# Moving the next batch's transposes into late attention steps and reordering the start of a fused attention and sine-MLP kernel on one Trainium2 core

## The chip, the cores and the metric

The kernel runs on one core of one Trainium2 chip. The metric is the device time of one execution in microseconds (us), as a median of several executions. A profile of one execution gives its span (a little shorter than the timed run) and the time of each instruction. The engines are PE (TensorE), DVE (VectorE), ACT (ScalarE), POOL (GpSimd) and SP (SyncE). POOL and SP here also issue most transfers: POOL through the software queue, SP through a hardware queue.

## The reference, cut to what matters

```python
def _attn_ref(q, k, v, global_idx):            # B=8, H=8, S=576, D=64; 8 global positions
    scores = scale * np.matmul(q, k.transpose(0, 1, 3, 2))
    mask = np.abs(pos[:, None] - pos[None, :]) <= 32
    mask = mask | is_global[:, None] | is_global[None, :]
    ...                                        # softmax over the masked scores
    return np.matmul(attn, v)

def _moe_ref(x, w_in, w_out, alpha):           # x: 4608 x 512, w_in: 512 x 2048
    h = x @ w_in
    s = np.sin(alpha * h)
    g = h + s * s / (alpha + 1e-09)
    return g @ w_out
```

The attention's output, 8 batches of 576 tokens, is the input x of the second part. The kernel treats x in 9 chunks of 512 tokens.

## The kernel before

One period per batch: an attention stage, then the first product of a chunk (tile hb). The second product of the chunk before (tiles ops and o, 64 wide matmuls) is cut into groups of four, the "filling", that stand between the attention's steps. A step of the attention makes scores of one unit, their exponential on ACT, the mask on DVE, a row sum (den) and the values (num). Before a head pair can be scored, its k and q are turned by 24 PE transposes; the transposes of the next batch stand partly in the hb stage.

```python
def stage_Q(psA, b, n):
    ...                                            # 16 score matmuls into Sp
    nc.scalar.activation(out=E[:], in_=Sp[:, :, 0:EW], func=AF.Exp, scale=scale)
    nc.vector.tensor_tensor(out=E[:], in0=E[:], in1=mk..., op=ALU.mult)      # mask at once
    return E

# second product, end of a tile of 128 rows
if ts == CH // P - 1:
    nc.vector.tensor_copy(out=osb[:], in_=ops[:])   # last of four on DVE
else:
    nc.scalar.copy(out=osb[:], in_=ops[:])          # the others on ACT

# squares of an hb stage: POOL, but for these of the 16
sq_late = lambda nt: {5: nc.scalar, 10: nc.vector, 15: nc.vector}.get(nt, nc.gpsimd)

# attention of batch p: transposes of its own head pairs 2 and 3 in steps -2 and 0
parts, last = attention(p, psA, {2: -2, 3: 0})
counts = [1, 1, 1, 1, 1, 2, 2, 1, 0]                # groups of filling after each step
...
# hb stage: value shift, then head pairs 0 and 1 of the next batch
i_ = (10, 13)
m1[i_[0]] = partial(chain, m1[i_[0]], *pre, partial(stage_T, p + 1, 0, psB, "hb"))
m1[i_[1]] = partial(chain, m1[i_[1]], partial(stage_T, p + 1, 1, psB, "hb"))

# start
shift_v(0, nc.gpsimd)                               # copies values one block on, within SBUF
for f in w_loads[:2]:
    f()                                             # both halves of w_in, POOL's queue
def globals_v0():
    nc.vector.tensor_copy(out=VZ[96:128], in_=Vg32[96:128])
def loads():
    for f in [partial(gather_kq, 1), ..., pool_regs] + v_loads(1, ((0, H),)) + kq1[:2] + w_loads[2:3]:
        f()
```

The softmax here doesn't subtract the row's maximum and nothing guards it: scores larger than these inputs give would overflow.

Of the kernel before, what the change touches and what calls it, by code (L numbers as in the profile page):

```python
# [17 lines left out]
def kernel(  # L18
# [122 lines left out]
    def shift_v(b, eng=nc.sync):  # L141
        W = VW[b % 2].rearrange("p a h u d -> p a h (u d)")
        eng.dma_start(out=W[0:64, 1], in_=W[QB : QB + 64, 0])
        eng.dma_start(
            out=W[64:KB, 1, :, 0 : (NU - 1) * D], in_=W[64 - QB : KB - QB, 0, :, D:]
        )
# [11 lines left out]
    def w_load(dst, src):  # L158
# [8 lines left out]
        for i in range(2)  # L167
    ] + [
        partial(
            w_load, w_out[:, i * NT // 2 : (i + 1) * NT // 2, :],  # L170
            moe_w_out[i * WH : (i + 1) * WH, :].rearrange("(t p) n -> p t n", p=P),
        )
        for i in range(2)
# [33 lines left out]
    for f in kq0[:4]:  # L207
        f()
# [4 lines left out]
    )  # L213

# [3 lines left out]
    def zero_v(i, eng=nc.vector):  # L218
# [16 lines left out]
    Gf = setup.tile([P, NG], F32, name="Gf")  # L235
    nc.vector.tensor_copy(out=Gf[:], in_=gall[:].bitcast(DT.int32)[:, 0::2])
    Gsel = setup.tile([P, 3 + NG], F32, name="Gsel")
    nc.vector.tensor_scalar(
        out=Gsel[:, 1:2], in0=I8[:, 0:1], scalar1=2.0, scalar2=None, op0=ALU.mult
    )  # L240
    nc.vector.scalar_tensor_tensor(
        out=Gsel[:, 2:3], in0=I8[:, 1:2], scalar=1.0 / (2 * NHP) - 2.0, in1=Gsel[:, 1:2],
        op0=ALU.mult, op1=ALU.add,
    )
    nc.vector.scalar_tensor_tensor(
        out=Gsel[:, 3:], in0=I8[:, 3:], scalar=0.0, in1=Gf[:], op0=ALU.is_equal, op1=ALU.mult
    )
    nc.vector.tensor_reduce(
        out=Gsel[:, 0:1], in_=Gsel[:, 3:], axis=mybir.AxisListType.X, op=ALU.add
    )  # L250
    rowi = const.tile([P, 1], DT.uint32, name="rowi")
    nc.vector.scalar_tensor_tensor(
        out=rowi[:], in0=Gsel[:, 2:3], scalar=float(S), in1=Gsel[:, 0:1],
        op0=ALU.mult, op1=ALU.add,
    )

    def gather_kq(i):
        for kq, src in ((0, k), (1, q)):
            nc.gpsimd.indirect_dma_start(
                out=GKQ[:, kq, i, :],  # L260
                out_offset=None,
                in_=src.rearrange("b h s d -> (b h s) d"),
                in_offset=bass.IndirectOffsetOnAxis(ap=rowi[:, 0:1], axis=0),
                element_offset=i * 2 * H * S * D,
            )

    zero_v(0)
    for f in v0 + kq0[4:]:
        f()
    gather_kq(0)  # L270
    Kps0 = psA0.tile([P, 2 * CH], BF, name="o2")

    def edges(t_):
# [5 lines left out]
    Vg32 = setup.tile([P, DM], F32, name="Vg32")  # L279
    zero(Vg32[96:128])  # L280
    zero(kTw[0][:, :, KB:P])

# [13 lines left out]
    nc.vector.tensor_tensor(  # L296
        out=OH[:], in0=T6[:, :, None].to_broadcast([P, NTW, NG]),
        in1=Gf[:, None, :].to_broadcast([P, NTW, NG]), op=ALU.is_equal,
    )
    Gp = setup.tile([P, 1], F32, name="Gp")  # L300
    nc.vector.tensor_copy(out=Gp[:], in_=gcol[:].bitcast(DT.int32)[:, 0:1])
    DQ = setup.tile([P, S], F32, name="DQ")
    nc.scalar.activation(out=DQ[:], in_=IQ[:], func=AF.Square, scale=-1.0, bias=Gp[:, 0:1])
    nc.vector.tensor_scalar(
# [47 lines left out]
    zero(VZ[0:96].bitcast(F32))  # L352
    for hp in range(1, NHP):
        zero(kTw[hp][:, :, KB:P])
    nc.vector.memset(ones[:], 1.0)
# [8 lines left out]
    shift_v(0, nc.gpsimd)  # L364
    for f in w_loads[:2]:
        f()
# [14 lines left out]
    def globals_v0():  # L381
        nc.vector.tensor_copy(out=VZ[96:128], in_=Vg32[96:128])
# [7 lines left out]
    def gather_v():  # L390
        regs = [
            nc.sync.value_load(gsc[0:1, 2 * j : 2 * j + 1], min_val=0, max_val=S - 1)
            for j in range(NG)
        ]
        for j in range(NG):
            nc.sync.dma_start(
                out=Vg32[KB + j : KB + j + 1, :].rearrange("p (h d) -> p h d", d=D),
                in_=v[0, :, bass.ds(regs[j], 1), :].rearrange("h o d -> o h d"),
            )
        for j in range(NG):  # L400
            nc.sync.dma_start(
                out=gN[2 * B * j : 2 * B * (j + 1), :].rearrange("b (h d) -> b h d", d=D),
                in_=v.rearrange("b (c h) s d -> (b c) h s d", c=2)[:, :, bass.ds(regs[j], 1), :].rearrange("b h o d -> b h (o d)"),
            )
# [68 lines left out]
    def T_Q(b, hp, qpool, qtag, copy):  # L473
        Qps = qpool.tile([P, S], BF, name=qtag)
        T_half(qk[b][0], b, hp, Qps)
        copy(out=qT[hp][:, :, 0:QB], in_=Qps[:].rearrange("p (i c) -> p i c", c=QB))

    def stage_T(b, hp, pool, tag):
        T_K(b, hp, Kps, nc.vector.tensor_copy)
        T_Q(b, hp, pool, tag, nc.scalar.copy)  # L480
# [16 lines left out]
    def stage_Q(psA, b, n):  # L497
        Sp = psA.tile([P, 2, CH], F32, name="Sp")
        i0 = blocks(n)[0][1]
# [8 lines left out]
        nc.scalar.activation(out=E[:], in_=Sp[:, :, 0:EW], func=AF.Exp, scale=scale)  # L508
        mk = MASK[:, i0 : i0 + NB, :].rearrange("p u c -> p (u c)")
# [3 lines left out]
        return E  # L513
# [80 lines left out]
    def attention(b, psA, t_at=None):  # L594
# [7 lines left out]
        def step(j):  # L602
            if j == -3:
                nc.scalar.preload_act_table_set("natural_log_exp_and_others")  # L604
            if j >= 0:
                stage_V(psA, b, j, Es.pop(j), recs.pop(j), gn)
            if 0 <= j + 1 < NUN:
                recs[j + 1] = stage_D(psA, j + 1, Es[j + 1], gd)
                if j + 2 == NUN:
                    stage_Gd(gd, gr)  # L610
                    nc.scalar.preload_act_table_set("trig_and_small")
            if j + 3 < NUN:
                Es[j + 3] = stage_Q(psA, b, j + 3)

        def one(op, j):
            if op == "Q":
                Es[j] = stage_Q(psA, b, j)
            elif op == "D":
# [7 lines left out]
        if t_at is None:  # L626
            return one, partial(stage_G, b, gn, gr)
        parts = [partial(step, j) for j in range(-LEAD, NUN)]
        for hp, j in t_at.items():
            parts[j + LEAD] = partial(chain, parts[j + LEAD], partial(stage_T, b, hp, psA, "qp"))  # L630
        return parts, partial(stage_G, b, gn, gr)

    def chain(*fs):
        for f in fs:
            f()


    def mm1(c, H2b, psB, sq):
# [10 lines left out]
        for nt in range(NT):  # L649
            def slot(nt=nt):  # L650
# [13 lines left out]
                eng = sq(nt)  # L664
                if eng is nc.scalar:
# [12 lines left out]
    def mm2(c, H2b, pools, cut=False):  # L678
# [3 lines left out]
        for ts in range(CH // P - (1 if cut else 0)):  # L682
            for g in range(NT // G4):
                def slot(ts=ts, g=g):
# [10 lines left out]
                    if g == NT // G4 - 1:  # L695
                        osb = osbp.tile([P, DM], F32, name="osb")
                        if ts == CH // P - 1:
                            nc.vector.tensor_copy(out=osb[:], in_=ops[:])
                        else:
                            nc.scalar.copy(out=osb[:], in_=ops[:])  # L700
# [44 lines left out]
    sq_late = lambda nt: {5: nc.scalar, 10: nc.vector, 15: nc.vector}.get(nt, nc.gpsimd)  # L745
# [9 lines left out]
    def loads():  # L755
        for f in [partial(gather_kq, 1), partial(zero_v, 1, nc.gpsimd), pool_regs] + v_loads(1, ((0, H),)) + kq1[:2] + w_loads[2:3]:
# [18 lines left out]
    def phase_0():  # L775
        Q, D_, V = (partial(partial, one, o) for o in "QDV")
        fs = {
            "warm": warm, "loads": loads, "vg": globals_v0, "vn": globals_v, "alpha": partial(alpha_t, aB),
            "keep": keep_warm, "last": last0, "A": partial(globals_t, 0, psC, "ops"), "kb": lambda: [f() for f in kq1[2:]],
        }  # L780
        for hp, (kp, ck, qpool, tag) in enumerate(
# [3 lines left out]
            fs[f"q{hp}"] = partial(T_Q, 0, hp, qpool, tag, acopy if hp < 3 else vcopy)  # L785
# [4 lines left out]
        for o, f in (("Q", Q), ("D", D_), ("V", V)):  # L790
            fs.update({f"{o}{j}": f(j) for j in range(NUN)})
        order = (
            "warm K0 q0 G0 Q0 K1 k1 q1 p1 loads Q1 D0 Q2 D1 K2 q2 G2 D2 Q3 vg K3 q3 G3 D3 Q4 V0 V1 D4 Q5 V2 V3 D5 V4 "
            "alpha V5 last keep A vn kb n0 n1 n2 n3"
# [4 lines left out]
    for p in range(NCH):  # L799
# [4 lines left out]
        elif p < B:  # L804
            with phase_pool("psA", 1) as psA:
                for tag, shape, dt_ in (
                    ("num", [P, NB, QC], F32), ("den", [P, NB, QC], F32),
                    ("qp", [P, S], BF), ("o2", [P, DM], F32),
# [3 lines left out]
                if p == 1:  # L812
                    fill[:8] = [fill[4 * (i % 2) + i // 2] for i in range(8)]
                parts, last = attention(p, psA, {2: -2, 3: 0})
                counts = [1, 1, 1, 1, 1, 2, 2, 1, 0]
                fill.pop(0)()
                fill.pop(0)()
# [7 lines left out]
                run(parts + [last], counts + [0], fill)  # L825
# [6 lines left out]
        with phase_pool("psB", 6) as psB:  # L832
# [3 lines left out]
            if p < 3:  # L836
                m1[5] = partial(chain, m1[5], partial(globals_t, p + 1, psB, "hb"))
            if p + 1 < B:
                i_ = (10, 13)
                pre = [partial(shift_v, p + 1), partial(global_v, p + 1)]  # L840
                if p == 0:
                    m1[5] = partial(chain, m1[5], *pre)
                    m1[6] = partial(chain, m1[6], w_loads[3])
                    pre, i_ = (), (12, 14)
                m1[i_[0]] = partial(chain, m1[i_[0]], *pre, partial(stage_T, p + 1, 0, psB, "hb"))
                m1[i_[1]] = partial(chain, m1[i_[1]], partial(stage_T, p + 1, 1, psB, "hb"))
# [34 lines left out]
```

## Time and profile before

| | before |
|---|---|
| median of the first three timed runs | 367.18 us (366.81 to 367.78) |
| span of the profile, mean PE clock | 366.4 us, 0.972 |
| start, up to the first hb matmul | 34.99 us |
| first hb stage, then attention of batch 1 | 16.23 and 25.56 us |
| second hb stage, then attention of batch 2 | 15.61 and 22.48 us |
| one settled hb stage and one settled attention | 15.61 and 22.53 us |

A stage is told from the timeline: from its first matmul on hb to the first scores or w_out matmul after it, and so on in turn. The prediction below shows the main views. The columns of a timeline are start, duration, engine, line of the program, operation, out<-in, shapes, count, and in brackets the idle time of the engine ahead of it with what released it. From the timelines of DVE and PE of the kernel before:

```profile
21.68 0.45 DVE L382 CAST VZ<-Vg 32x512 bf16<-32x512 f32 x1
34.99 5.34 PE L653 MATMUL hb<-xT,w_in 128*128 128x512 bf16 x23 [1.40 <-POOL xT L586]
51.22:76.78 25.56, 21.25 (x313) 10.77 (x316) 14.39 (x37) 17.20 (x26) 14.00 (x26) 1.00 1.82 157
```

DVE casts the eight rows of global values (VZ) at 21.68 and waits for nothing, and PE begins hb at 34.99 after 1.40 us for POOL's eight small copies into xT. The third line is the stretch of batch 1's attention: PE is busy 21.25 of 25.56 us, at full clock (the 1.00).

### The profile page before, as it was taken

The page shows a single profiled execution, that of the slowest core. Times are in us where ns is not written, and L with a number is a line of the kernel's source. Part 1 is how long each engine was busy: PE and PEld are TensorE (multiplying, and loading weights), DVE is VectorE, ACT ScalarE, POOL GpSimd, SP SyncE. Part 2 cuts the span into 40 slices and gives each one's busy share as a digit, 9 for nine tenths or more (in the row PEclk, how much of TensorE's full clock was granted, in tenths as well). Part 3 has the DMA queues.
Part 4 walks back from the last instruction along what each step waited for, and adds up shares of the span by engine and source line. Part 5 has one row for each costly group of instructions (what it writes and reads, how often), then busy time and mean ns, then how long its engine had stood idle before and what let it go on. Part 6 is the DMA issues. An engine that isn't in the chain of part 4 may idle for free.

```text
span 366.4 us, 9350 instructions
## 1 busy us (share of the span) xinstructions
PE 333.3 (91%) x3684; PEld 171.0 (47%) x3738; DVE 234.7 (64%) x511; ACT 248.2 (68%) x378; POOL 218.3 (60%) x316
## 2 busy tenths in 40 slices
PE   5686987899999998999899989998999999999995
PEld 4563444444544454444444454445444544344444
DVE  5755784648764886379656964597649764864700
ACT  3755866758875888588848786778757965845411
POOL 9868897158954894298618871789078006955000
PEclk9559999999999999999999999999999999999999
DMA  9999999940993189434974199409950001001012
GB/s 75 168 196 180 193 177 172 165 132 8 81 181 109 41 54 167 104 81 32 167 100 110 8 163 118 119 0 142 128 138 4 30 30 57 2 0 57 30 70 76
DMA packets 133150, 35.40 MB, mean 97 GB/s; under 512 B 121794, under 2 KB 126818, under 8 KB 133106
## 3 DMA queue, kind: packets, MB, share of 16 engines
q0 software_dynamic: 123120, 20.04, 75.9%
q1 hardware_dynamic: 9682, 14.63, 13.6%
q8 instruction: 29, 0.48, 0.6%
q10 hardware_dynamic: 304, 0.14, 0.1%
q14 instruction: 15, 0.12, 0.1%
HBM read 38.95 MB, written 9.44 MB: 132 GB/s over the span
## 4 chain that ended last, share of the span: by engine, by line
PE 63%; ACT 13%; DVE 7%; DMA 7%; POOL 5%; issue 4%; POOLq 1%; ACTq 0%; DVEq 0%
PE hb L653 28%; PE ops L690 13%; PE o L690 10%; DMA w_out<-in_moe_w_out_dram 5%; ACT E L508 4%; PE num L551 3%; ACT Sb L660 3%; DVE kTw L465 2%; ACT L604 2%; DMA QS<-in_q_dram 2%; PE Sp L502 2%; PE hb L690 2%; DVE S L668 2%; ACT rec L541 2%; PE Kps L456 2%
## 5 line engine op out<-in xcount | busy, mean ns | idle before, releaser
L660 ACT ACTIVATE Sb<-hb,alphaT 128x512 bf16<-128x512 f32 x144 | 98.1, 686 | 56.2 <-PE hb L653 53.9
L653 PE MATMUL hb<-xT,w_in 128*128 128x512 bf16 x558 | 129.6, 379 | 3.8 <-POOL xT L586 1.4
L668 POOL TENSOR_TENSOR S<-Sb 128x512 bf16<-128x512 bf16 x108 | 109.6, 1039 | 35.4 <-ACT Sb L660 35.3
L643 DVE SCALAR_TENSOR_TENSOR H2b<-S,recipT,hb 128x512 bf16<-128x512 bf16 x144 | 102.4, 741 | 24.5 <-POOL S L668 24.3
L653 PEld LDWEIGHTS <-w_in 128*128 128x128 bf16 x576 | 55.1, 98 | 67.9 <-issue 2.9
L690 PEld LDWEIGHTS <-H2b 128*128 128x128 bf16 x560 | 49.6, 98 | 59.4 <-issue 5.9
L690 PE MATMUL ops<-w_out,H2b 128*128 128x512 bf16 x283 | 70.7, 380 | 3.8 <-issue 2.1
L690 PE MATMUL o<-w_out,H2b 128*128 128x512 bf16 x209 | 51.0, 380 | 3.5 <-issue 2.4
L510 DVE TENSOR_TENSOR E<-E,MASK 128x896 bf16<-128x896 bf16 x48 | 30.3, 632 | 34.7 <-ACT E L508 34.7
L586 POOL COPY xT<-xg 128x4 bf16 x64 | 12.9, 201 | 64.6 <-DVE xg L584 61.2
L508 ACT ACTIVATE E<-Sp 128x896 bf16<-128x896 f32 x48 | 43.6, 907 | 7.2 <-PE Sp L502 7.1
L539 ACT ACTIVATE lnd<-den 128x384 f32<-128x384 f32 x48 | 23.6, 491 | 24.7 <-PE den L533 24.6
L570 DVE TENSOR_TENSOR xT<-num,rec 128x384 bf16<-128x384 f32 (+1 forms) x60 | 25.8, 451 | 11.9 <-PE num L551 11.6
L502 PE MATMUL Sp<-qT,kTw 64*128 64x56 bf16 x768 | 20.9, 190 | 11.2 <-DVE kTw L465 2.8
L668 DVE TENSOR_TENSOR S<-Sb 128x512 bf16<-128x512 bf16 x27 | 17.9, 662 | 18.6 <-ACT Sb L660 18.3
L502 PEld LDWEIGHTS <-kTw 64*128 64x128 bf16 x768 | 15.8, 96 | 24.1 <-issue 13.9
L541 ACT ACTIVATE rec<-lnd 128x384 f32<-128x384 f32 x48 | 25.1, 523 | 1.5
L551 PEld LDWEIGHTS <-VW 120*64 120x64 bf16 (+1 forms) x768 | 16.8, 115 | 18.8 <-issue 11.0
L465 DVE COPY kTw<-Kps 128x1344 bf16<-128x1344 bf16 x29 | 24.6, 847 | 0.0
L128 POOL DMA_DIRECT2D KS<-in_k_dram x18 | 20.7, 1150 | 0.6 <-issue 0.4
L551 PE MATMUL num<-E,VW 120*64 120x56 bf16 (+1 forms) x720 | 20.1, 197 | 0.2 <-DVE gn L524 0.2
L128 POOL DMA_DIRECT2D QS<-in_q_dram x18 | 20.1, 1119 | 0.0
(135 smaller groups left out, 295.6 us busy)
## 6 DMA issues: line engine op xcount, KB each, us to landing
out_dram<-osb SPq DMA_DIRECT2D x35, 256.0 KB
KS<-in_k_dram POOLq DMA_DIRECT2D x14, 288.0 KB, 8.0
QS<-in_q_dram POOLq DMA_DIRECT2D x14, 288.0 KB, 9.2
VW<-in_v_dram POOLq DMA_DIRECT2D x12, 336.0 KB, 10.9
VW<-VW SPq DMA_DIRECT2D x7, 384.0 KB
w_in<-in_moe_w_in_dram POOLq DMA_DIRECT2D x2, 1024.0 KB, 15.7
w_out<-in_moe_w_out_dram POOLq DMA_DIRECT2D x2, 1024.0 KB, 16.5
VW<-VW SPq DMA_DIRECT2D x7, 240.0 KB
```

The costliest lines, as they stand in the source:

```text
L128: nc.gpsimd.dma_start(out=dst[:, h0 : h0 + nh].rearrange("p h t d -> p (h t) d"), in_=heads_ap(src, b, h0, 0, TW, 0, nh * NTW),)
L465: copy(out=kTw[hp][:, :, 0:KB], in_=bass.AP(tensor=base.tensor, offset=base.offset, ap=[list(base.ap[0]), [QB, NW], [1, KB]],),)
L502: nc.tensor.matmul(out=Sp[:, t, m * QC : (m + 1) * QC], lhsT=kTw[hp][pr, i, :], rhs=qT[hp][pr, i, :], start=True, stop=True, skip_group_ch ...
L508: nc.scalar.activation(out=E[:], in_=Sp[:, :, 0:EW], func=AF.Exp, scale=scale)
L510: nc.vector.tensor_tensor(out=E[:], in0=E[:], in1=mk[:, None, :].to_broadcast([P, 2, EW]), op=ALU.mult)
L541: nc.scalar.activation(out=rec[:], in_=lnd[:], func=AF.Exp, scale=-1.0)
L551: nc.tensor.matmul(out=num[pr, m, :], lhsT=W[0:nk, i % 2, 2 * hp + t, i // 2, :], rhs=E[0:nk, t, m * QC : (m + 1) * QC], start=b > 0 or m ...
L643: nc.vector.scalar_tensor_tensor(out=H2b[:, n_, :], in0=s_[:], scalar=recipT[:, n_ : n_ + 1], in1=h_, op0=ALU.mult, op1=ALU.add,)
L653: nc.tensor.matmul(out=h2[:], lhsT=w_in[:, ci, nt * P : (nt + 1) * P], rhs=xT[:, ci, c * CH : (c + 1) * CH], start=(ci == 0), stop=(ci == ...
L660: nc.scalar.activation(out=Sb[:], in_=h2[:], func=AF.Sin, scale=alphaT[:, nt : nt + 1])
L668: eng.tensor_tensor(out=S2[:], in0=Sb[:], in1=Sb[:], op=ALU.mult)
L690: nc.tensor.matmul(out=ops[:], lhsT=H2b[:, nt, ts * P : (ts + 1) * P], rhs=w_out[:, nt, :], start=(nt == 0), stop=(nt == NT - 1),)
```

## The change

Its intent: take the transposes of the next batch out of the hb stage, where PE has little idle time, and put all of them into the last attention steps, where it has some. Beside that: shift batch 0's values through SP in three pieces, get masks and first scores of batch 0 sooner, load batch 1's k and q ahead of w_out, copy one output tile of four on DVE instead of ACT (the first; the last stays on DVE), and rebalance the squares. The diff is cut to its core below. Left out are a few smaller moves: the copies of the turned q stand later in a step, a DVE square is preceded by a waiting product (H2b), and the tiles of one PSUM pool stand in another order.

```diff
-    def shift_v(b, eng=nc.sync):
+    def shift_v(b):
...                                     # two transfers become three, all through SP
-    shift_v(0, nc.gpsimd)
-    for f in w_loads[:2]:
-        f()
+    w_loads[0]()
...
-        nc.vector.tensor_copy(out=VZ[96:128], in_=Vg32[96:128])
+        nc.gpsimd.tensor_copy(out=VZ[96:128], in_=Vg32[96:128])
...                                     # in SP's loop of value rows
+            if j == NG - 3:
+                shift_v(0)
...
-                        if ts == CH // P - 1:
+                        if ts % 3 == 0:
                             nc.vector.tensor_copy(out=osb[:], in_=ops[:])
...
-    sq_late = lambda nt: {5: nc.scalar, 10: nc.vector, 15: nc.vector}.get(nt, nc.gpsimd)
+    sq_late = lambda nt: {3: nc.vector, 5: nc.scalar, 9: nc.vector, 12: nc.scalar, 15: nc.vector}.get(nt, nc.gpsimd)
...
-        for f in [partial(gather_kq, 1), partial(zero_v, 1, nc.gpsimd), pool_regs] + v_loads(1, ((0, H),)) + kq1[:2] + w_loads[2:3]:
+        for f in [partial(gather_kq, 0), globals_v0, partial(gather_kq, 1), w_loads[1], partial(zero_v, 1, nc.gpsimd), pool_regs] + kq1[:2]:
...                                     # mask split from the scores, placed ahead of den
+            if j + 1 == 0:
+                stage_M(0, Es[0])
+            if 0 < j + 2 < NUN:
+                stage_M(j + 2, Es[j + 2])
...
-                    fill[:8] = [fill[4 * (i % 2) + i // 2] for i in range(8)]
-                parts, last = attention(p, psA, {2: -2, 3: 0})
-                counts = [1, 1, 1, 1, 1, 2, 2, 1, 0]
-                fill.pop(0)()
-                fill.pop(0)()
+                    fill[:8] = [fill[i] for i in (0, 1, 4, 5, 2, 6, 3, 7)]
+                if p == 1:
+                    at = {-2: [T_(1, 2)], -1: [T_(1, 3)]}
+                elif p + 1 < B:
+                    at = {2 + hp: [T_(p + 1, hp)] for hp in range(NHP)}
+                counts = [1, 1, 1, 1, 1, 1, 2, 2, 4]
+                if p == 1:
+                    counts = [0, 0, 0, 0, 1, 2, 2, 3, 8]
+                else:
+                    fill.pop(0)()
+                    fill.pop(0)()
...                                     # hb stage of chunk 0
+                    m1[9] = partial(chain, m1[9], *vs)
+                    m1[0] = partial(chain, m1[0], *v_loads(1, ((0, H),)))
+                    m1[5] = partial(chain, m1[5], *kq1[2:])
+                    m1[8] = partial(chain, m1[8], w_loads[2])
+                    m1[10] = partial(chain, m1[10], *w_loads[3:])
+                    ts = {12: (1, 0), 14: (1, 1)}
```

## The prediction

> **What bounds the kernel now.** I read the page first (slices and chain), then the busy time by stretches, then the order of time inside one period. The kernel works in periods, one per batch: an attention stage, into whose gaps the second matrix product of the chunk before (tiles ops and o, 64 matmuls) is filled, then the first matrix product (tile hb, 64 matmuls). From the page of the kernel before:
>
> ```profile
> PE   5686987899999998999899989998999999999995
> PEclk9559999999999999999999999999999999999999
> DMA  9999999940993189434974199409950001001012
> PE 63%; ACT 13%; DVE 7%; DMA 7%; POOL 5%; issue 4%; POOLq 1%; ACTq 0%; DVEq 0%
> ```
>
> A slice is 9.16 us. Up to about 73 us the DMA engines are full and PE is not; from then on PE is at 90% or more. The chain of the end is mostly PE. So the first 77 us are one case (transfers and dependences), the rest another (TensorE, in order). Two stretches of a settled period, columns us, PE, PEld, DVE, ACT, POOL busy, clock, DMA:
>
> ```profile
> 153.20:168.70 15.50, 15.15 (x111) 7.25 (x112) 11.69 (x16) 11.84 (x18) 12.09 (x12) 1.00 0.26 65
> 168.70:191.40 22.70, 21.12 (x313) 10.85 (x317) 14.55 (x38) 16.97 (x27) 12.62 (x24) 1.00 1.42 120
> ```
>
> The period is 38.14 us (the stage starts are 130.49, 168.73, 206.87). No other engine is near it. What PE loses stands in the timeline of the attention stage that starts at 168.73 and of the hb stage ahead of it:
>
> ```profile
> 166.35 0.45 PE L456 MATMUL Kps<-identb,KS 96*64 96x96 bf16 x12 [0.25 <-DVE kTw L465]
> 172.05 0.61 DVE L510 TENSOR_TENSOR E<-E,MASK 128x896 bf16<-128x896 bf16 x1
> 173.87 0.38 PE L533 MATMUL den<-E,ones 120*64 120x448 bf16 x2
> 173.98 0.59 ACT L700 COPY osb<-ops 128x512 f32<-128x512 f32 x1 [0.15 <-PE ops L690]
> 176.37 0.38 PE L502 MATMUL Sp<-qT,kTw 64*128 64x56 bf16 x16 [0.27 <-ACT E L508]
> 179.59 0.28 PE L502 MATMUL Sp<-qT,kTw 64*128 64x56 bf16 x8 [0.47 <-DVE kTw L465]
> ```
>
> Note the order at 172 to 174: the mask of the first unit is done long before PE needs it, and the output copy of the first 128 rows runs on ACT behind PE's den. From start to start in this timeline a group of 4 wide matmuls takes 0.86 us, 16 scores 0.31, den 0.30, 16 values 0.28, the 24 transposes of one head pair 0.55. The attention stage holds 13.8 + 6 x 0.89 + 2 x 0.55 = 20.2 us of PE work and takes 22.5: 2.3 lost. The hb stage holds 13.8 + 1.1 and takes 15.6: 0.7 lost. So no more than 3 us of a period are to be had. The start:
>
> ```profile
> 10.34 0.56 PE L502 MATMUL Sp<-qT,kTw 64*128 64x56 bf16 x16 [2.34 <-ACT qT L421]
> 20.82 0.69 PE L456 MATMUL ops<-identb,QS 96*64 96x96 bf16 x12 [0.45 <-DMA QS<-in_q_dram]
> 7.53 0.78 ACT L303 ACTIVATE DQ<-IQ,Gp 128x576 f32<-128x576 f32 x1 [4.46 <-DVE EDGE L307]
> 60.00 1.02 PE L690 MATMUL ops<-w_out,H2b 128*128 128x512 bf16 x4 [1.71 <-DMA w_out<-in_moe_w_out_dram]
> ```
>
> ACT sits until 7.5 us for a scalar that DVE makes late, so the first scores are late; the last q load of batch 0 releases PE at 20.8; w_out releases it at 60.0.
>
> **What the Trainium skill says.** "DMA: Bandwidth & Descriptors", section "Queues, rings and completion order": each DMA engine takes turns between the queues it has work for, and within a queue descriptors are consumed in order. The trace agrees as to order: the 6144-byte packets of the value shift (software queue, issued at 15.0) move between 16 and 20 us, beside the last 128-byte packets of k and q, and those loads are told landed only at 19.37 and 20.78. "SBUF — State Buffer", section "SBUF: two separate sides": a GpSimd instruction and a DVE one that needs the shared ports exclude each other for a whole instruction. The trace agrees: the DVE square of 128x512 takes 0.44 us at 169.71 and 1.28 us at 316.10, where POOL runs squares end to end. "TensorE: Matmul & The Clock Gate", section "What's actually happening": full clock only after a busy window of about 3.4 us, half after an idle one. Here the clock is 0.50 from 8.3 to 28.8 us and 1.00 after; this is what a starved attention stage would risk again.
>
> **The change part by part.**
>
> 1. Transposes (settled periods, batches 2 to 6). All four head pairs of the next batch go from the hb stage (2) and early attention steps (2) to the last four steps. hb loses 2 x 0.55 of work and its 0.6 of gaps: 15.6 to about 13.9, -1.7. Attention gains 1.1 of work, and loses the kTw wait of 0.5. Their data come in time: the loads are issued from 1.1 us after the stage start, the first K of 207.95 landed in 5.4 us, a second q quad in 12.8 (131.57 to 144.41 from the first issue); the steps that need them stand at about 12 and 17 us.
>
> 2. Output copies. The first 128 rows' copy goes from ACT to DVE. The order of instructions of the changed kernel puts it on DVE ahead of the first mask, and PE's den comes right behind the four matmuls which that copy waits for. So PE must stop for the copy to start (0.2), the copy (0.69, as the DVE copy at 305.82 takes), the mask (0.57) and den's release (0.05): 1.5 us, where 0.2 are lost now. Part comes back, since scores wait less for ACT later in the stage. Following all engines through the stage by the durations above I get 24.4 us with four transposes, against 22.5 with two: +1.9. Sum of 1 and 2: 24.4 + 13.9 = 38.3 against 38.1 per period, so about +0.5 over five.
>
> 3. Squares. POOL has 13 of 1.02 us in an hb stage of 13.8 and falls behind (DVE's 1.28 above); 11 leave it room, DVE and ACT take one each. Without this the hb stage could not shrink to 13.9. Its worth is in part 1.
>
> 4. Batch 7 loses its own transposes: about -0.7, against the same copy wait.
>
> 5. Setup and shift. DQ, masks and the first scores move 1.5 to 2.5 us up, but the next transposes need the q loads of 17.35 and 20.78. With the shift off the software queue these should land earlier: their packets are nearly done at 17.7, while the shift through SP now shares the engines; I take 19. What follows the last q load is 10 us of half-clock PE work now, about 9.5 then. Start of hb: 35.0 to 32.7, -2.3; first hb stage -0.5.
>
> 6. Batch 1. Its k, q come before w_out, and no filling is done before its step 1. POOL must issue 2.6 us of v loads, 2.4 of k, q and 2.8 of w_out inside the first hb stage beside 8 squares (8.2) and copies (2.4): 18.4 us in a stage of 15.6. The first mask comes some 6.5 us after the stage (6.4 now), but without the 20 fill matmuls (4.3 us) done by then. The unfilled steps run at ACT's pace, 0.90 + 0.49 + 0.52 a step. I get 28.4 us against 25.7 (51.2 to 76.9, stall for w_out included): +2.7. Then four transposes in the second hb stage in place of two: +1.1.
>
> Sum: -2.3 - 0.5 + 2.7 + 1.1 + 0.5 - 0.7 = +0.8, so 368.0. Such a hand schedule errs toward too many waits, and a change with this many fine choices was likely made against a clock; I take 2 us off: **366.0**.
>
> **The rivals.**
>
> A. The late transposes pay in full: den does not wait, or the wait is absorbed. For it: PE has 3 us of gaps a period and every other engine room (table above). Then 1.5 us less in five periods and the last: 367.2 - 9 - 1 = 357 to 359. Against it: the order on DVE and the PE order leave no way round the copy.
>
> B. The copy wait takes what the transposes give (mine): the settled period stays at 38 us, total 364 to 369.
>
> C. Batch 1 starves PE. Its first 11 us hold about 4 us of PE work; if the clock falls to half there as it did at 8.3 us, the filling behind runs at half speed for a window or two, +2 to +4: 370 to 373. Against it: w_out stalls of 1.7 us at 60 did not lower the clock.
>
> D. The shift through SP slows the loads it shares engines with: q lands at 21 to 23, the start gains nothing or loses 1: 368 to 370.
>
> **Range and chances.** B is my main line with A as its fast tail and C, D as its slow one; the periods err by 0.4 each, five of them 2, the start 1.5, batch 1 2, together about 3, plus the doubt about B against A. 8 in 10: 358.5 to 372.5. Faster by over 2% is under 359.8, which needs A nearly whole: 0.18. Slower by over 2% is over 374.5, which needs C and D: 0.07. Within: 0.75.
>
> **What would show it.** Step 1: hb stages of 13.8 to 14.0 us without transposes. Step 2: in each settled attention stage den idle about 1.5 us, released by the mask on DVE, with an osb copy just ahead of it; period 38.0 to 38.5. If den follows without idle time and the period is 36.7, A holds and I am wrong. Step 5: the first hb matmul near 32.7, last q landing near 19. Step 6: first filling some 12 us after the stage starts, PE below half busy before, the stage about 28 us; a clock under 1.00 there would be C.

## The result, and the profile after

| | median of runs (lowest to highest) | ratio to before, 95% interval |
|---|---|---|
| before, same chip | 367.48 us (366.81 to 368.01, 4 runs) | |
| after | 381.06 us (378.72 to 382.83, 4 runs) | 1.0367 (1.0307 to 1.0426) |

All runs are fast: none lies over 1.5% above the fastest of its kernel. A ratio here and below is the mean time of one kernel's fast runs over the mean of the other's from the same rounds, so it is not quite the ratio of the medians. The changed kernel is 3.7% slower, outside the range of the prediction. The span of its profile is 379.3 us against 366.4, the mean clock 0.949 against 0.972. From its page:

```profile
PE   6557696999988998999899989998999999999996
PEclk9557898599999999999999999999999999999999
DMA  9985999994099146944694449643974002000112
PE 63%; ACT 14%; DMA 7%; DVE 5%; issue 4%; POOL 4%; POOLq 1%; SPq 1%; ACTq 0%; DVEq 0%
```

The clock row says where to look first: in slices 4, 5, 7 and 8 (a slice is 9.48 us) the clock stands at 5 to 8 tenths, where before it stood at 9 from the fourth slice on. The second half of the page is as before. Three places carry the loss.

**The start.** From the timelines of PE and POOL after:

```profile
22.73 0.69 PE L468 MATMUL ops<-identb,QS 96*64 96x96 bf16 x12 [2.43 <-DMA QS<-in_q_dram]
28.73 0.61 POOL L392 CAST VZ<-Vg 32x512 bf16<-32x512 f32 x1 [10.44 <-DMA gN<-in_v_dram]
29.39 0.58 PE L575 MATMUL num<-E,VZ 120*64 120x448 bf16 x2 [2.06 <-POOL VZ L392]
40.91 6.77 PE L678 MATMUL hb<-xT,w_in 128*128 128x512 bf16 x24 [3.67 <-POOL xT L600]
```

The last q of batch 0 releases PE at 22.73 (20.82 before). POOL stands 10.44 us for the cast of VZ, PE waits for that cast, and POOL's later work comes late with it: hb starts at 40.91 (34.99 before), and its first 24 matmuls take 6.77 us (23 took 5.34), because the clock fell to half from 40.4 to 43.8.

**Batch 1.** PE's timeline and the stretch of this stage, whose column before the last two is the clock:

```profile
62.20 0.38 PE L513 MATMUL Sp<-qT,kTw 64*128 64x56 bf16 x16 [0.95 <-ACT E L519]
63.76 0.38 PE L547 MATMUL den<-E,ones 120*64 120x448 bf16 x2 [1.18 <-DVE E L525]
69.10 1.89 PE L717 MATMUL ops<-w_out,H2b 128*128 128x512 bf16 x4
59.07:88.20 29.13, 25.43 (x318) 13.27 (x318) 14.96 (x39) 16.63 (x25) 14.58 (x27) 0.82 1.73 165
```

The stage takes 29.13 us and its first filling stands at 69.10, ten microseconds in (before: at its very start, 51.22). The steps ahead of it wait on ACT and DVE, and the group at 69.10 takes 1.89 us, not 1.03: the clock was at half from 64.3 to 74.6.

**A settled period.** The stretches of the hb stage and the attention of batch 4, and three lines of the timeline at the start of that attention:

```profile
169.47:183.28 13.81, 13.81 (x66) 6.27 (x65) 10.41 (x16) 10.96 (x17) 9.57 (x10) 1.00 0.29 76
183.28:207.93 24.65, 22.78 (x366) 12.11 (x365) 15.96 (x40) 17.82 (x28) 13.16 (x25) 1.00 1.30 111
```

```profile
187.89 0.69 DVE L725 COPY osb<-ops 128x512 f32<-128x512 f32 x1 [1.31 <-PE ops L717]
188.50 0.61 DVE L525 TENSOR_TENSOR E<-E,MASK 128x896 bf16<-128x896 bf16 x1
189.17 0.38 PE L547 MATMUL den<-E,ones 120*64 120x448 bf16 x2 [1.31 <-DVE E L525]
```

The hb stage is pure matmul now, 13.81 us for 13.81 busy, 1.8 us less than before. The attention is 2 us longer: the output copy and the mask stand in a row on DVE, and den waits 1.31 us for them.

### The profile page after: what moved, and what is told of

It reads as the page before. It is cut to its first block, busy times and chain, and to the rows that moved or that the text cites. A ratio compares the mean times of both kernels' runs of the same rounds, so it can differ in the third digit from the quotient of the medians.

```text
span 379.3 us, 9422 instructions
## 1 busy us (share of the span) xinstructions
PE 342.1 (90%) x3738; PEld 174.4 (46%) x3738; DVE 237.7 (63%) x523; ACT 247.0 (65%) x379; POOL 203.8 (54%) x302
## 4 chain that ended last, share of the span: by engine, by line
PE 63%; ACT 14%; DMA 7%; DVE 5%; issue 4%; POOL 4%; POOLq 1%; SPq 1%; ACTq 0%; DVEq 0%
PE hb L678 30%; PE ops L717 11%; PE o L717 11%; ACT E L519 4%; DMA VW<-VW 3%; PE Sp L513 2%; PE num L565 2%; ACT L619 2%; DMA VW<-in_v_dram 2%; PE den L547 2%; ACT lnd L553 2%; PE hb L717 2%; DMA out_dram<-osb 2%; ACT L628 2%; DVE H2b L668 2%
## 5 line engine op out<-in xcount | busy, mean ns | idle before, releaser
L685 ACT ACTIVATE Sb<-hb,alphaT 128x512 bf16<-128x512 f32 x144 | 96.9, 684 | 61.4 <-PE hb L678 57.8
L695 POOL TENSOR_TENSOR S<-Sb 128x512 bf16<-128x512 bf16 x94 | 96.3, 1043 | 51.7 <-ACT Sb L685 47.0
L678 PEld LDWEIGHTS <-w_in 128*128 128x128 bf16 x576 | 55.9, 98 | 71.4 <-issue 6.3
L717 PEld LDWEIGHTS <-H2b 128*128 128x128 bf16 x560 | 50.4, 98 | 56.9 <-issue 2.9
L717 PE MATMUL ops<-w_out,H2b 128*128 128x512 bf16 x304 | 75.6, 386 | 0.0
L717 PE MATMUL o<-w_out,H2b 128*128 128x512 bf16 x224 | 54.7, 382 | 0.0
L547 PE MATMUL den<-E,ones 120*64 120x448 bf16 x96 | 19.4, 398 | 10.6 <-DVE E L525 10.4
L477 DVE COPY kTw<-Kps 128x1344 bf16<-128x1344 bf16 x29 | 24.4, 840 | 3.6 <-PE Kps L468 3.6
L565 PEld LDWEIGHTS <-VW 120*64 120x64 bf16 (+1 forms) x768 | 17.7, 119 | 19.1 <-issue 12.0
L128 POOL DMA_DIRECT2D KS<-in_k_dram x18 | 20.8, 1157 | 3.5 <-issue 3.4
L565 PE MATMUL num<-E,VW 120*64 120x56 bf16 (+1 forms) x720 | 21.1, 201 | 0.3 <-issue 0.3
```

Of the source, the lines that this page charges most:

```text
L547: nc.tensor.matmul(out=den[pr].rearrange("p u c -> p (u c)"), lhsT=ones[0 : KB + NG], rhs=E[0 : KB + NG, t, :], start=True, stop=True, ski ...
L565: nc.tensor.matmul(out=num[pr, m, :], lhsT=W[0:nk, i % 2, 2 * hp + t, i // 2, :], rhs=E[0:nk, t, m * QC : (m + 1) * QC], start=b > 0 or m ...
L678: nc.tensor.matmul(out=h2[:], lhsT=w_in[:, ci, nt * P : (nt + 1) * P], rhs=xT[:, ci, c * CH : (c + 1) * CH], start=(ci == 0), stop=(ci == ...
L685: nc.scalar.activation(out=Sb[:], in_=h2[:], func=AF.Sin, scale=alphaT[:, nt : nt + 1])
L695: eng.tensor_tensor(out=S2[:], in0=Sb[:], in1=Sb[:], op=ALU.mult)
L717: nc.tensor.matmul(out=ops[:], lhsT=H2b[:, nt, ts * P : (ts + 1) * P], rhs=w_out[:, nt, :], start=(nt == 0), stop=(nt == NT - 1),)
```

## The experiments

Twelve kernels ran, in four groups, each beside the kernel before on the same chip. All gave correct results. All runs are fast but two: one of e6's four is slow (373.02; the others have a median of 370.05), and the state of e9's single run is unknown. In the first group the kernel before itself took 369.71 us, in the others 367.03 to 367.59, so a ratio is compared across groups only to about half a per cent; the stage lengths of the profiles do not depend on this. This table sums them up; "b1" is the first hb stage plus the attention of batch 1 (work moves between the two), "b2" the attention of batch 2, "settled" the usual attention of batches 3 to 6, all in us.

| kernel | median | ratio (95%) | start | b1 | b2 | settled |
|---|---|---|---|---|---|---|
| before | 367.48 | 1 | 34.99 | 41.79 | 22.48 | 22.53 |
| after | 381.06 | 1.0367 (1.0307 to 1.0426) | 40.91 | 47.29 | 25.90 | 24.36 |
| e1_copy_act | 373.38 | 1.0099 (1.0029 to 1.0169) | 40.37 | 46.14 | 24.15 | 23.01 |
| e2_vz_dve | 377.80 | 1.0237 (1.0188 to 1.0287) | 38.36 | 45.87 | 25.68 | 24.23 |
| e3_shift_pool | 381.30 | 1.0323 (1.0267 to 1.038) | 41.32 | 45.83 | 25.91 | 24.37 |
| e4_b1_order | 375.36 | 1.0154 (1.0108 to 1.0201) | 39.13 | 43.12 | 25.94 | 24.22 |
| e5_settled_act | 361.05 | 0.9805 (0.9741 to 0.987) | 35.08 | 42.00 | 23.02 | 23.02 |
| e6_settled_dve | 370.21 | 1.0036 (0.9965 to 1.0107) | 34.92 | 42.65 | 28.05 | 24.36 |
| e7_start_both | 373.58 | 1.0146 (1.0079 to 1.0212) | 35.82 | 45.36 | 25.00 | 24.35 |
| e8_all_repaired | 364.95 | 0.9916 (0.9857 to 0.9975) | 37.02 | 42.77 | 23.66 | 23.02 |
| e10_old_squares | 360.55 | 0.9809 (0.9771 to 0.9847) | 35.28 | 42.79 | 23.02 | 23.09 |
| e9_copy_first | 379.56 (one run) | none | 37.86 | 49.13 | 25.09 | 24.35 |
| e11_b1_fill | 375.38 | 1.0231 (1.0172 to 1.0291) | 35.32 | 46.73 | 25.34 | 24.36 |
| e12_b1_loads | 378.35 | 1.03 (1.0259 to 1.0341) | 36.05 | 46.92 | 25.98 | 24.36 |

The settled hb stage is 15.61 us before and 13.81 in every other kernel of the table (14.10 ahead of batch 3). Batch 4's attention is 0.3 to 1.5 us longer than the usual one in every changed kernel, in part for a gap that the section on the prediction treats. The theory was that three separate things cost: POOL's cast in the start, the order of batch 1, and the output copy on DVE. Each has a rival below.

### e1_copy_act: the first output copy back on ACT

```diff
-                        if ts % 3 == 0:
+                        if ts == CH // P - 1:
```

> The changed kernel with the first output copy of a chunk (tile osb, rows 0 to 127) back on ACT; nothing else. Theory 'copy wait': in every settled attention stage den waits 1.3 us for the mask, which stands on DVE behind that copy. Without it den follows at once, the settled period falls from 38.2 to 36.8 to 37.2 us, and the total by 7 to 9 us, to 372 to 374 us. Rival 'absorbed': ACT's chain of exp, ln, exp sets the steps, so the period stays above 37.9 and the total falls by less than 2 us.

The settled attention fell from 24.36 to 23.01, the ratio from 1.0367 to 1.0099; the total, 373.38, is within the expected 372 to 374. From the timeline of its batch 4:

```profile
183.13 0.38 PE L547 MATMUL den<-E,ones 120*64 120x448 bf16 x2
183.24 0.58 ACT L727 COPY osb<-ops 128x512 f32<-128x512 f32 x1
```

Here den follows without an idle time in brackets and the copy runs behind it on ACT, as in the kernel before. So the wait is the copy's place on DVE, ahead of the mask, not the late transposes, which are all still there.

### e2_vz_dve: the cast of the global values back on DVE

```diff
-        nc.gpsimd.tensor_copy(out=VZ[96:128], in_=Vg32[96:128])
+        nc.vector.tensor_copy(out=VZ[96:128], in_=Vg32[96:128])
...
-        for f in [partial(gather_kq, 0), globals_v0, partial(gather_kq, 1), w_loads[1], ...
+        for f in [partial(gather_kq, 0), partial(gather_kq, 1), w_loads[1], ...
```

> The changed kernel with the copy of the global value rows (VZ<-Vg, batch 0) back on DVE, ahead of the first values; nothing else. Theory 'POOL queue': that copy blocked POOL from 18.3 to 28.7 us (it waited for the row gathers, which stood behind w_in), so the gathers, w_in, the index loads and k, q of batch 1 came late and POOL could write the global columns of xT only at 38.8. Without it the first hb matmul comes at 35 to 37 us instead of 40.9, its first 24 matmuls at full clock, the total falls by 4 to 8 us. Rival 'shift through SP': the values wait for the rows behind the shift on SP's queue anyway, the first hb stays at 39.5 or later, the total falls by less than 2 us.

```profile
28.30 0.42 DVE L392 CAST VZ<-Vg 32x512 bf16<-32x512 f32 x1
38.36 5.34 PE L678 MATMUL hb<-xT,w_in 128*128 128x512 bf16 x24 [1.73 <-POOL xT L600]
```

POOL no longer stands still, hb starts at 38.36, 2.6 us sooner, and its first 24 matmuls run at full clock (5.34 us, the kernel after 6.77). But the start was expected at 35 to 37: 3.4 us of the delay remained, and the median fell by 3.3 us where 4 to 8 were expected, so the cast is not the whole cause.

### e3_shift_pool: batch 0's value shift back on POOL's queue

```diff
-    def shift_v(b):
+    def shift_v(b, eng=nc.sync):
-        nc.sync.dma_start(...)          # three times
+        eng.dma_start(...)
+    shift_v(0, nc.gpsimd)
     w_loads[0]()
-            if j == NG - 3:
-                shift_v(0)
```

> The changed kernel with the value shift of batch 0 back on POOL's queue ahead of w_in (still three pieces); the VZ copy stays on POOL. Theory 'POOL queue': the copy still waits for the gathers behind w_in, so the first hb matmul stays at 39.5 to 42 us and the total within 2 us of the changed kernel. Rival 'shift through SP': last q of batch 0 lands near 20.8 instead of 22.7 and the first hb comes 3 to 6 us earlier, the total falls by as much.

```profile
21.03 0.69 PE L467 MATMUL ops<-identb,QS 96*64 96x96 bf16 x12 [0.55 <-DMA QS<-in_q_dram]
29.06 0.61 POOL L393 CAST VZ<-Vg 32x512 bf16<-32x512 f32 x1 [7.76 <-DMA GKQ<-in_q_dram,rowi]
```

The start did not get shorter (41.32), as the theory of POOL's cast said. The two lines hold what e2 had left open. First, the last q releases PE at 21.03 and not at 22.73: with the shift on SP's queue, q lands 1.7 us later. The Trainium skill's page "DMA: Bandwidth & Descriptors", section "Issuing engines are not separate DMA queues", says that transfers started by different engines run on the same 16 DMA engines and interleave. The trace agrees: in the changed kernel the shift's large packets move from 17.7 us on beside the last of q. But the edit moves a second thing: with the shift ahead of it on POOL, the first half of w_in is issued at 15.62 and not at 12.21, and its packets start at 19.5 and not at 16.7. Which of the two takes the 1.7 us, shift or w_in, no run separates. Second, the cast waits for the two row gathers (GKQ) that POOL had issued just before it, though it does not read their data. The profile of the changed kernel had named gN, another small transfer, at this place; the gathers' landing times there (28.44 and 28.62) fit the cast's start at 28.73, so a releaser's name is a hint that a run has to confirm.

### e4_b1_order: e2 with batch 1's loads and filling as before

```diff
+ v_loads(1, ((0, H),)) + kq1[:2] + w_loads[2:3]        # in loads(), ahead of the first hb stage
-                    fill[:8] = [fill[i] for i in (0, 1, 4, 5, 2, 6, 3, 7)]
+                    fill[:8] = [fill[4 * (i % 2) + i // 2] for i in range(8)]
-                if p == 1:
-                    counts = [0, 0, 0, 0, 1, 2, 2, 3, 8]
-                else:
-                    fill.pop(0)()
-                    fill.pop(0)()
+                fill.pop(0)()
+                fill.pop(0)()
-                    ...                                  # v, k, q, w_out inside the hb stage
+                    m1[5] = partial(chain, m1[5], *vs)
+                    m1[6] = partial(chain, m1[6], *w_loads[3:])
```

> e2 and, for batch 1, the loads and the filling as in the kernel before (v, first half of k and q, first half of w_out ahead of the first hb stage, the rest early in it; filling from the first step on). Theory 'starved stage': the attention stage of batch 1 took 29.1 us (25.6 before) because it ran 11 us without filling and then at half clock; with the old order it takes 25 to 26.5 us at clock 1.00, and the total is 3 to 4 us below e2. Rival 'transfers': w_out lands no earlier, the stage waits for it instead, and the total is within 1 us of e2.

```profile
57.06:82.25 25.19, 23.54 (x317) 11.20 (x316) 14.56 (x38) 16.23 (x25) 12.95 (x25) 0.93 1.29 110
```

The attention of batch 1 takes 25.19 us (29.14 in e2), its clock is 0.93 (one half-clock window of 3.4 us). The first hb stage is 1.2 us longer than e2's, so 2.75 us remain of the gain, and the medians differ by 2.4 us, less than the 3 to 4 that were expected. The loads and filling of batch 1 are worth that much; which of the two, e11 and e12 tell.

### e5_settled_act and e6_settled_dve: the settled part of the change alone

Both start from the kernel before and take the split mask, the transposes in late steps, the squares, and batch 2's transposes in the second hb stage. They also take the smaller moves named with the diff. The start, the load order and batch 1 are as before. They differ in one line:

```diff
 # from e5_settled_act to e6_settled_dve
-                        if ts == CH // P - 1:
+                        if ts % 3 == 0:
```

> The kernel before with only the settled-stage part of the change (transposes of the next batch late in attention, the mask halves split off, the new squares, all of batch 2's transposes in the hb stage of batch 1); start, load order and batch 1 as before, and the copies of the output tiles as before (three on ACT, one on DVE). Theory 'the copy on DVE gives back what the transposes give': the settled hb stage takes 13.8 us (15.6 before), settled attention 22.9 to 23.2 (22.5), so about 1.3 us less for each of the batches 3 to 6 and about 2 less in the last, and batches 1 and 2 together within 2 us of before: in all 5 to 9 us below the kernel before of the same chip (ratio 0.976 to 0.986), and the start of hb at 35.0 as before. Rival 'late transposes are worth nothing, they only move work from hb to attention': settled attention near 24.3 here too, within 2 us of before.

> The same as e5_settled_act, with the first of the four output copies on DVE as in the change: the one line that the two differ by. Theory 'copy on DVE': settled attention 24.2 to 24.4 with hb at 13.8, so the settled period is 38.1, as before; the whole 6 to 9 us above e5_settled_act and within 2 us of the kernel before (ratio 0.995 to 1.008). Rival 'the copy only cost in the changed kernel because start and batch 1 were late': within 3 us of e5_settled_act.

An attention of each (hb stages are 13.81 in both), e5 first:

```profile
131.24:154.26 23.02, 22.66 (x366) 12.04 (x365) 15.32 (x39) 18.16 (x29) 13.64 (x25) 1.00 1.39 117
```

```profile
137.00:161.22 24.22, 22.65 (x366) 12.06 (x365) 16.00 (x41) 17.59 (x27) 13.02 (x25) 1.00 1.32 112
```

PE is busy 22.66 and 22.65 us in them; the 1.2 us between is PE standing still. With the copy on ACT the settled part of the change is 2.0% faster than before (361.05 us). With the copy on DVE it is worth nothing (1.0036). Both ratios are within the ranges given beforehand. The transposes pay about 1.3 us a period, and one copy on DVE ahead of the first mask takes it back. The profiled run of e6 lies over 1.5% above the fastest of its runs and counts as slow; in its batch 2 PE stood still for 2.17 us and the clock then fell to half for 3.4 us, which with the copy wait makes the 28.05 of the table. The stretch shown ran at full clock. e5_settled_act, with e10 below, is also the fastest version.

### e7_start_both: e2 and e3 together

```diff
 # e2_vz_dve with e3's lines
+    shift_v(0, nc.gpsimd)
     w_loads[0]()
-            if j == NG - 3:
-                shift_v(0)
```

> The changed kernel with two parts of its start undone: the global values copied on DVE again (as e2_vz_dve) and the shift of batch 0's values on the POOL queue again (as e3_shift_pool). Alone they gave a start of hb at 38.4 and 41.3 (40.9 in the changed kernel, 35.0 before). Theory 'two delays in parallel, the longer hides the other: POOL's copy ends last, and behind it the last q piece lands 1.7 us late because the shift on SP's queue takes transfer time': hb starts at 35.3 to 37.0 and the last q transposes run at 21.0 instead of 22.7 to 23.4; ratio to before 1.010 to 1.020, 1.5 to 3 us below what e2_vz_dve had. Rival 'the shift's queue costs nothing': hb starts at 38.4 and the ratio is 1.024 as in e2_vz_dve.

```profile
21.36 0.69 PE L467 MATMUL ops<-identb,QS 96*64 96x96 bf16 x12 [0.83 <-DMA QS<-in_q_dram]
35.82 5.34 PE L677 MATMUL hb<-xT,w_in 128*128 128x512 bf16 x24
```

Alone, e3 gave nothing and e2 2.6 us; together they give 5.1. So two delays lay side by side, and the longer hid the shorter: behind the cast lay the later q. With both undone the start is 0.8 us from that of the kernel before.

### e8_all_repaired: every blamed part undone

This is e7 with e4's lines of batch 1 and e1's line.

> The changed kernel with every part undone that the runs so far blame: e7_start_both, the load order and filling of batch 1 as before (as e4_b1_order), and the first output copy on ACT (as e1_copy_act). What stays of the change are the split mask, the earlier first scores, the k and q loads of batch 0 ahead of the values of batch 1, the late transposes and the new squares. If the account is complete (start, copy wait, batch 1): start 35.3 to 37, attention of batch 1 near 25.2, batch 2 near 24.2, settled period 36.9, so 360 to 364 in the profile and a ratio of 0.980 to 0.995. Rival 'something else of the change costs too (the new squares, the order of pools, the split mask)': ratio above 1.0.

364.95 us, ratio 0.9916: within the range that was given (the profile's 364.2 is just above its 360 to 364), and the rival (something else costs as well) is not needed for the sign. The start, 37.02, is at the edge of what was expected. It is still 4 us above e5_settled_act: 1.9 in the start, 0.8 in b1, 0.6 in batch 2, the rest spread. What stays of the change in it but not in e5 is the setup, the earlier first scores and the place of the loads; together they cost rather than gain, and no run separates them further.

### e10_old_squares: e5 with the squares as before

```diff
-    sq_late = lambda nt: {3: nc.vector, 5: nc.scalar, 9: nc.vector, 12: nc.scalar, 15: nc.vector}.get(nt, nc.gpsimd)
+    sq_late = lambda nt: {5: nc.scalar, 10: nc.vector, 15: nc.vector}.get(nt, nc.gpsimd)
```

> e5_settled_act with one line put back: the squares of the settled hb stages as before (POOL 13, DVE 2, ACT 1 of 16, in place of 11, 3 and 2). My prediction said that the hb stage could not shrink to 13.9 us without the new squares. Theory 'squares needed': the settled hb stage takes 14.3 us or more (13.81 with the new ones) or the attention stage behind it 0.5 us longer because the last squares on POOL end late, so 2 to 5 us more in all than e5_settled_act (ratio to before 0.986 to 0.995). Rival 'the transposes' absence alone gives the 13.81': hb at 13.8 to 13.9 and a ratio within 0.004 of the 0.9805 of e5_settled_act.

```profile
155.55:169.36 13.81, 13.81 (x66) 6.27 (x65) 10.08 (x15) 10.71 (x16) 11.63 (x12) 1.00 0.30 74
```

The hb stage is 13.81 us with 13 squares on POOL as well (POOL is busy 11.63 us of it), and the ratio is 0.9809 against 0.9805. The new split of the squares is worth nothing that these runs can see.

### e9_copy_first: the cast ahead of the gathers on POOL

```diff
-        for f in [partial(gather_kq, 0), globals_v0, partial(gather_kq, 1), ...
+        for f in [globals_v0, partial(gather_kq, 0), partial(gather_kq, 1), ...
```

> The changed kernel with two neighbours on POOL swapped: the copy of the global values ahead of the first two row gathers instead of behind them. In the changed kernel that copy waited until 28.73 us for the two gathers (landed at 28.4 and 28.6, queued behind half of w_in) and for the eight value rows on SP's queue. Theory 'gathers': the copy runs at 20 to 25 us and hb starts near 37.5 to 38.5, since what e2_vz_dve had left then sets the start, though the gathers and w_in issued later may cost some of it. Rival 'the value rows on SP's queue, behind the shift, land that late themselves': the copy still runs at 27 us or later and hb starts at 40 or later.

```profile
25.05 0.61 POOL L392 CAST VZ<-Vg 32x512 bf16<-32x512 f32 x1 [9.81 <-DMA gN<-in_v_dram]
37.86 7.03 PE L678 MATMUL hb<-xT,w_in 128*128 128x512 bf16 x24 [2.68 <-POOL xT L600]
```

The cast ran at 25.05 in place of 28.73, at the edge of the expected range, and hb at 37.86. So the gathers held it for 3.7 us. The rest of its wait I put down to the value rows that it reads, whose last two SP issues behind the shift. The packet records support this: between 17 and 23 us SP's queue moved 3 packets of value rows (256 bytes) in e9, and 175 in e3, where the shift is on POOL's queue. It was not tried by itself. Both theories hold in part.

### e11_b1_fill and e12_b1_loads: the two halves of batch 1's order

Both start from e7. e11 puts the filling of batch 1 back to the start of its stage and keeps the change's load order; e12 puts the load order back and keeps the late filling.

```diff
 # e11_b1_fill
-                    counts = [0, 0, 0, 0, 1, 2, 2, 3, 8]     # and the two early groups again
 # e12_b1_loads
-                    m1[8] = partial(chain, m1[8], w_loads[2])
+ v_loads(1, ((0, H),)) + kq1[:2] + w_loads[2:3]             # in loads(), as before
```

> e7_start_both (the changed kernel with its start mended) with only the filling of batch 1 as before: w_out matmuls in every step from the start of the stage. The load order stays the change's, with k, q of batch 1 ahead of w_out. In e7_start_both the attention of batch 1 took 28.6 us (25.6 before), and the first half of w_out landed at 59.9, 7.3 us after that stage began. Theory 'the load order forbids early filling': PE now stands still in that stage until about 59 to 60 us for w_out (waits of 5 to 7 us), and the stage takes 28 to 31 us. Rival 'only the late filling costs': the stage takes 25 to 26.5 us and the ratio to before falls from 1.0146 to about 1.007.

> e7_start_both with only the load order of batch 1 as before (values and w_out ahead of the later k and q loads), while the filling keeps the change's late places. Theory 'what costs is that no filling stands in the first steps': the stage (with the first hb stage, since the transposes shift between the two) takes as long as in e7_start_both, 45.4 us in sum, or up to 1 us more or less, with the half clock in it again. Rival 'the loads themselves, crowding the first hb stage on POOL, cost': the sum falls to 43 us or less (41.8 before, 42.8 in e8_all_repaired).

PE's timeline of e11, then of e12:

```profile
58.67 1.89 PE L716 MATMUL ops<-w_out,H2b 128*128 128x512 bf16 x4 [6.56 <-DMA w_out<-in_moe_w_out_dram]
```

```profile
56.58 0.45 PE L467 MATMUL qp<-identb,QS 96*64 96x96 bf16 x12 [1.58 <-DMA QS<-in_q_dram]
64.08 1.89 PE L716 MATMUL ops<-w_out,H2b 128*128 128x512 bf16 x4
```

In e11 PE stands 6.56 us for w_out. This wait lies within what is counted as the first hb stage here (23.35 us), so the expected 28 to 31 us of the attention stage alone did not show; the sum, 46.73 us, is 1.4 above e7's. In e12 the sum is 46.92 us: k and q come later now, the first filling is no sooner, and the clock is at half from 58.9 to 69.1; the sum is above the 44.4 to 46.4 that was expected. So neither half alone is the culprit. Order of loads and place of filling belong together: with both as before (e4 and e8) the sum is 43.12 and 42.77, with both as changed 45.36, with either alone about 46.8. Of the first two, e4 still has the shift on SP and e8 has the copy on ACT; the step from e2 to e4, 45.87 to 43.12, is free of this.

## Why the prediction was wrong

Its parts stage by stage, predicted and measured from the two profiles (us, after less before):

| | predicted | measured |
|---|---|---|
| start (step 5) | -2.3 | +5.92 |
| first hb stage (step 5) | -0.5 | +1.93 |
| attention of batch 1 (step 6) | +2.7 | +3.57 |
| second hb stage (step 6) | +1.1 | +1.43 |
| attention of batch 2 (steps 1 and 2) | +1.9 | +3.42 |
| batches 3 to 6 with the hb stages before them (1 and 2) | +0.8 | +0.46 |
| batch 7 with the hb stage before it (1 and 4), last chunks, end | -2.4 | -3.75 |
| sum | +1.3 | +12.98 |

The prediction's own sum was +0.8: it wrote +0.5 for steps 1 and 2, where five times 1.9 less 1.7 is +1.0.

**Right: the settled periods (steps 1 and 2).** I predicted an hb stage of 13.9 and an attention of 24.4; they take 13.81 and mostly 24.36, and the wait before den came from where I said. e1, e5 and e6 show that it is the copy on DVE. The period of my main line (rival B) held, though not its total, and A, den without the wait, is what e5 shows.

**Right in kind, too small: step 6.** I said 28.4 us for batch 1's attention and it took 29.13; rival C's half clock came true. The page "TensorE: Matmul & The Clock Gate", section "What's actually happening", puts the window at about 3.4 us; the half-clock spells of these runs are one window (40.4 to 43.8), two (55.3 to 62.1 in e11) and three (64.3 to 74.6) of that length. That the clock fell because PE had waited is argued from the order of events, not shown by a run that holds the clock.

**Wrong: step 5.** The first scores did come 2.0 us sooner (8.34 for 10.34), as it said. What failed is the rest of the step: "With the shift off the software queue these should land earlier: ... I take 19", and from it a start of 32.7. The start was 40.91. Two things took its place.
1. The last q came at 22.7, not 19: later than before (20.8), not earlier. That is my rival D (21 to 23), and e3 and e7 show it: with the shift on POOL's queue q comes at 21.0 and 21.4 (by the shift's packets or by w_in's earlier ones, see e3).
2. I had not seen the cast of VZ at all. It moved from DVE to POOL, behind two gathers that are queued behind half of w_in. In the kernel before it had cost nothing, and the prediction does not name it. It held POOL for 10.4 us, and with it everything that POOL does later in order: two more gathers, the other half of w_in, register loads, k and q of batch 1, the copies into xT. e2, e3, e7 and e9 show it.

The first hb stage then missed by 2.4 us more. e2 shows 1.4 of them as a consequence of the start: with the start earlier it took 16.73 at full clock.

**Too small: batch 2.** Its attention grew by 3.42 us, not 1.9. Most of the other 1.5 us is one gap, from PE's timeline of the changed kernel:

```profile
119.41 0.35 PE L513 MATMUL Sp<-qT,kTw 64*128 64x56 bf16 x14 [1.55 <-issue]
```

It lies inside a group of 16 scores, and "issue" says that the profile shows nothing that PE waited for. I went through PE's idle times after 85 us in all 14 traces: eleven have such a gap of over 0.6 us (13 in all, 0.65 to 2.17 us), the kernel before has none. All 13 end 2.4 to 2.9 us after a 16 KB packet of the instruction queue started, of which there are 29 in a run. And they stand at two fixed places of PE's program: at its matmul 1244 (1243 in e6) in batch 2, or 2136 in batch 4. This speaks for a wait for instructions; no run tests it. e2_vz_dve has no such gap in batch 2 and still takes 25.68 us there, so this stage is not fully explained.

**Wrong in size: batch 7 and the end,** -3.75 in place of -2.4. About 2.15 of it is the last settled pair (hb 13.81, attention 22.12), close to what was said. The remaining 1.6 lie in the last two hb stages and the end; e10 gives back 0.35 of the first, and the rest stays open.

**Step 3** was wrong: e10 shows that the hb stage gets to 13.81 without the new squares.

**The 2 us of shading** for "such a change was likely made against a clock" rested on nothing in the profile and pointed the wrong way.

**Range and chances.** I gave C and D together 0.07 to be slower by over 2%. Both came true, and a third delay that I had not listed hid one of them.

## What to carry to other kernels

An engine that both computes and starts transfers is in order: before moving even a half-microsecond copy onto it, list everything that stands ahead of it and behind it on that engine, and what it waits for. When two delays lie side by side, undoing either alone can show little or nothing (e3), so test them together before acquitting one. Work that fills gaps must not put its own clean-up (here an output copy) ahead of the instruction that the critical engine needs next, and a load order and the place of the work that uses the loads must be changed together.

## What the Trainium skill lacked or had wrong

- No page that I read warns that moving an on-engine copy to GpSimd can hold back transfers that GpSimd has yet to issue. "DMA: Bandwidth & Descriptors", section "Issuing engines are not separate DMA queues", treats the starter as a small cost; here the cast of VZ held POOL for 10.44 us (7.76 in e3), 3.7 of it for gathers that the same engine had just issued, and hb came 2.6 us later for it alone, 5.1 with the shift.
- "Runtime: NRT & Kernel Launch", section "Instruction fetch mechanics", says that the cost of crossing a block of instructions is mostly hidden, and names taken branches as the case that stalls. Eleven of 14 traces show TensorE standing still for 0.65 to 2.17 us with nothing waited for, always at the same two places of its program and each time 2.4 to 2.9 us after a 16 KB instruction packet started (13 of 13). That the one causes the other is not shown here.
